# Loads of 48 and 40 partition rows are issued as loads of 32 and 8 rows in a gated linear recurrence kernel

## The chip, the core and the metric

The kernel runs on one core of a Trainium2 chip. A core has a matrix engine (PE, with its weight loads shown as PEld), a vector engine (DVE), a scalar engine (ACT), a general engine (POOL) and a queue engine (SP) that here does nothing but issue DMAs. The 16 DMA engines of the core carry all transfers between the chip's main memory and the on-chip memory of 128 partitions. The metric is the device time of one execution in microseconds (us).

## What is computed

The reference takes `r, k, v, w, a, b` of shape (4 batches, 8 heads, 768 steps, 40) and runs a recurrence over the steps, per batch and head, on a 40 x 40 state. The result goes through a small gated network.

```
for t in range(S):
    y[:, :, t] = einsum('bhd,bhde->bhe', rt, state)
    Sa = einsum('bhde,bhe->bhd', state, at)
    state = state * wt[:, :, None, :] - einsum('bhd,bhe->bhde', Sa, bt) \
            + einsum('bhd,bhe->bhde', vt, kt)
...
h = maximum(x @ w_in, 0);  u, v = halves of h
v_n = (v - mean) / sqrt(var + 1e-6)
out = (u * (w_spatial @ v_n + b_spatial)) @ w_out
```

## The kernel before

The 768 steps are cut into chunks of 64, and the four batches into two pairs, so that 24 chunks (numbered s or q, 0 to 23) run one after the other. A chunk holds 16 (batch, head) pairs. Eight of them lie on partitions 0 to 39 and eight on partitions 64 to 103, one partition for each of the 40 features; the code calls these two sets the halves, `par` 0 and 1.

For every chunk four inputs are loaded, all of them issued by SP:

- `ein` (line 556, `prep_load`): w, a, b and k of the chunk, 2064 numbers (8256 bytes) for each partition. There are two such tiles, used by turns. The host array has 64 rows for each half. Rows 40 to 63 hold constants (w is 1, the rest 0), and the vector engine's scans run over all 128 partitions. The loads of chunks 4 to 23 take 48 rows of each half. Those of chunks 0 to 3 are made another way at the start, and also fill the rows above 40 (or a memset does).
- `lin` (line 760, `lin_load`): v and r of the chunk, 40 rows for each half, 8 pieces of 512 bytes each.
- `lisw` (line 764): a part of r again, with the halves exchanged, 40 rows.
- `Rt` (line 768): v again in another layout, 64 rows.

The vector engine starts a chunk with `scan1` (line 569), a running product over w, which reads `ein`; `scan2` (578), `at` (596) and `sl` (602) read it too, after which the next load but one may overwrite the tile. PE first reads `lin` in `b_h` (line 816).

SP also issues the stores and reloads that carry results along: `scr` and `scn` (lines 590 and 923, decay factors between chunks), `xs` (1057, the recurrence's output), and, from about 270 us on, the transfers of the gated network, which runs interleaved with the later chunks: `xt` (1076 and 1080), `uts` (1160) and `vns` (1143).

The order of the instructions on every engine, SP included, is written out beforehand: a table of times sorts the steps, and each engine runs its list in that order. What stands behind a waiting instruction waits too. Each DMA adds to one of eight semaphores, DMAHW0 to DMAHW7, taken in rotation, and the program makes a DMA wait until the one issued eight places earlier has landed. So SP has at most eight transfers on their way.

Of the kernel before, what the change touches and what calls it, by code (L numbers as in the profile page):

```python
# [22 lines left out]
E = 40  # L23
# [8 lines left out]
LATE = 2 * C  # L32
# [465 lines left out]
def phase1(ctx, tc, early, late, vtok, win, xs, vns, uts, dscr):  # L498
    nc = tc.nc
# [4 lines left out]
    PR = (LO, HI)  # L504
    RR = (slice(0, E), slice(64, 64 + E))
    LV = slice(0, 64 + E)

    def pool(name, bufs=1, **kw):
        return ctx.enter_context(tc.tile_pool(name=name, bufs=bufs, **kw))
# [34 lines left out]
    lin = [linp.tile([P, NU, LATE + E], F32, name=f"lin{i}") for i in range(2)]  # L544
# [7 lines left out]
    def prep_load(s, rows, cols=slice(0, EW), i=None, queues=(nc.sync, nc.sync)):  # L552
        t = ein[s % 2 if i is None else i]
        for par in range(2):
            o = par * 64
            queues[par].dma_start(out=t[o:o + rows, cols], in_=early[par, s, 0:rows, cols])

    def scan1(s, i=None):
        t = ein[s % 2 if i is None else i]
        Et = etp.tile([P, WF], F32, name="Et")  # L560
        at = fifo[s % 8].tile([P, NU, C], F32, name="at")
        sl = fifo[s % 8].tile([P, NU, 2, C], F32, name="sl")
        wseg = t[:, 0:WF]
        oth = t[:, WF:].rearrange("p (q n c) -> p n q c", q=3, c=C)
        sx = pin.tile([P, WF], F32, name="S", bufs=2)
        sv = sx.rearrange("p (n c) -> p n c", c=WSEG)
        st["pre", s] = (Et, at, sl)
        st["raw", s] = (wseg, oth, sv)
        nc.vector.tensor_tensor_scan(  # L569
            out=sx[:, ::-1], data0=wseg[:, ::-1], data1=ends[:, ::-1],  # L570
            initial=0.0, op0=ALU.mult, op1=ALU.add,
        )
        nc.vector.reciprocal(out=eseg[:, :, 0:1], in_=sv[:, :, 1:2])

    def scan2(s):
        Et, at, sl = st["pre", s]
        wseg, oth, sv = st["raw", s]
        nc.vector.tensor_tensor_scan(
            out=Et, data0=wseg, data1=ends, initial=0.0, op0=ALU.mult, op1=ALU.add,
        )  # L580
# [11 lines left out]
    def at_mul(s, eng, ns=slice(0, NU)):  # L592
        Et, at, sl = st["pre", s]
        oth = st["raw", s][1]
        Ev = Et.rearrange("p (n c) -> p n c", c=WSEG)
        eng.tensor_tensor(out=at[:, ns], in0=oth[:, ns, 0], in1=Ev[:, ns, 0:C], op=ALU.mult)

    def sl_mul(s, eng, ns=slice(0, NU)):
        Et, at, sl = st["pre", s]
        wseg, oth, sv = st["raw", s]  # L600
        k = ns.stop - ns.start
        eng.tensor_tensor(  # L602
            out=sl[:, ns], in0=oth[:, ns, 1:],
            in1=sv[:, ns, 2:C + 2].unsqueeze(2).broadcast_to([P, k, 2, C]), op=ALU.mult,
        )
# [151 lines left out]

    def lin_load(s):
        for par in range(2):
            nc.sync.dma_start(out=lin[s % 2][RR[par], :, 0:LATE], in_=late[par, s])  # L760

    def lin_load_swapped(s):
        for par in range(2):
            nc.sync.dma_start(out=lisw[s % 2][RR[1 - par], :, 0:C], in_=late[par, s, :, NP:NU, C:2 * C])

    def vtok_load(s):
        for par in range(2):
            nc.sync.dma_start(out=Rts[s % 2][par][PR[1 - par], :, C:], in_=vtok[s, par])
# [243 lines left out]
    def c_mp_out(s, g):  # L1012
# [5 lines left out]
        mp = st["xx", g][:, :, C:]  # L1018
        sc = st["scn"][LV, g].rearrange("p e n -> p n e")
        if s in ADD_PE:  # L1020
            nc.vector.tensor_tensor(out=Mc[LV, gp, 0:E], in0=mp[LV], in1=sc, op=ALU.mult)
            return
        mn = Mc[:, gp, 0:E]
        nc.vector.tensor_tensor(out=mn[LV], in0=mp[LV], in1=Mc[LV, gp, 0:E], op=ALU.add)
        nc.vector.tensor_tensor(out=Mc[LV, gp, 0:E], in0=mn[LV], in1=sc, op=ALU.mult)

# [11 lines left out]
    def c_y_out(s, g):  # L1038
# [3 lines left out]
        if c % 2 == 0:  # L1042
# [3 lines left out]
        nc.vector.tensor_tensor(  # L1046
            out=y[LV, :, ys], in0=st["bp", g][LV, :, 0:C], in1=Ev[LV, gp, 0:C], op=ALU.mult,
        )
# [118 lines left out]
    def at(fn, *args, name=None):  # L1167
        plan.append((next(left[name or fn.__name__]) / 1e4, len(plan), fn, args))
# [46 lines left out]
    for q in range(GS, NS):  # L1215
        for fn in (scan1, scan2, scr_store, lprime, lblock):
            at(fn, q)
        at(at_mul, q, AT_ENG)
        at(sl_mul, q, SL_ENG)
        if q + 2 < NS:  # L1220
            at(prep_load, q + 2, 48)
    for g in range(1, NS // GS):
        gen = invert16(g) if g < N16 else invert(g)
        for k in range(INV_N[g]):
# [28 lines left out]
    def pads(eng, t):  # L1253
        w = t[:, 0:WF].rearrange("p (n c) -> p n c", c=WSEG)
        eng.memset(w[:, :, 1:C + 1], 1.0)
        eng.memset(w[:, :, 0:C + 2:C + 1], 0.0)
        eng.memset(t[:, WF:], 0.0)

    with tc.manual_schedule():
        W, O = slice(0, WF), slice(WF, EW)  # L1260
        qs = (nc.sync, nc.scalar)
        nc.vector.memset(eseg[:, :, 0:C + 1], 0.0)
        nc.vector.memset(eseg[:, :, C + 1:], 1.0)
        pads(v, ein[1])
        p.memset(maskl, -1.0)
        for q in range(P // HB):
            rows = slice(q * HB, (q + 1) * HB)
            p.affine_select(
                out=maskl[rows], in_=maskl[rows], pattern=[[1, HB]], base=0,
                channel_multiplier=-1, compare_op=ALU.is_gt, fill=0.0,  # L1270
            )
        pads(p, ein[2])
        pads(p, ein[3])
        for q in range(GS):
            for cols in (W, O):
                prep_load(q, 48 if q else 64, cols, q, qs)
        lin_load(0)
        lin_load_swapped(0)
        vtok_load(0)
        make_identity(nc, ident)  # L1280
        for t in (Mc, *xfs):
            p.memset(t, 0.0)
        for q in range(2):
            for rows in RR:
                diag = ident[rows, rows.start:rows.start + E]
                nc.scalar.activation(
                    lin[q][rows, :, LATE:], diag.unsqueeze(1).broadcast_to([E, NU, E]), AF.Copy
                )
                nc.scalar.activation(
                    lisw[q][rows, :, C:], diag.unsqueeze(1).broadcast_to([E, NP, E]), AF.Copy  # L1290
                )
        for q in range(GS):
            scan1(q, q)
            scan2(q)
            at_mul(q, v)
            sl_mul(q, v)
            scr_store(q)
            lprime(q)
            if q:
                lblock(q - 1)  # L1300
            if q == 0:
                b_copy(0, 0)
                b_copy(0, 1)
            if q == 1:
                b_lka(0)
                b_tok(0, 0)
                b_tok_out(0, 0)
            if q == 2:
                b_lka_out(0, 0)
                b_lka_out(0, 1)  # L1310
                b_tok(0, 1)
                b_tok_out(0, 1)
                b_l21(0)
                b_l21_out(0)
        lblock(GS - 1)
        lin_load(1)
        lin_load_swapped(1)
        vtok_load(1)
        prep_load(4, 48)
        prep_load(5, 48)  # L1320
        b_h(0)
        for _ in (invert16 if N16 else invert)(0):
            pass
        b_h_out(0, 0)
        b_h_out(0, 1)
        p.memset(lowrow, 1.0)
        p.memset(half, 0.0)
        for q in range(P // HB):
            rows = slice(q * HB, (q + 1) * HB)
            p.affine_select(  # L1330
                out=lowrow[rows], in_=lowrow[rows], pattern=[[0, 1]], base=-QB,
                channel_multiplier=1, compare_op=ALU.is_ge, fill=0.0,
            )
            for blk in range(2):
                cols = slice(blk * QB, (blk + 1) * QB)
                nc.scalar.activation(
                    half[rows, blk, cols], ident[rows, q * HB + blk * QB:q * HB + (blk + 1) * QB], AF.Copy,
                )
        open_fifo()
        st["dec"] = late_bufs.enter_context(tc.tile_pool(name="dec", bufs=1))  # L1340
        at(b_zt, 0)
        at(b_zt_out, 0)
        prep(0)
        at(b_x21, 0)
        at(b_x21_out, 0)
        plan.sort()
        anchors = {}
        n = 0
        while plan[n][0] < NS:
            t, _, fn, args = plan[n]  # L1350
            for a, _ in W_PLAN:
                if t >= a and a not in anchors:
                    anchors[a] = mark(nc)
            fn(*args)
            n += 1
# [59 lines left out]
```

## Time and profile before

| | |
|---|---|
| median of 3 runs | 685.62 us (680.43 to 688.12) |
| the profiled execution's own time | 683.68 us |
| its span, first to last instruction | 681.9 us |
| PE busy | 87% of the span |
| DVE busy | 77% |
| ACT, POOL busy | 62%, 32% |
| moved by DMA | 83.42 MB, mean 122 GB/s |
| mean granted PE clock | 0.885 of full speed |

The profile has several views. The page gives busy times, and the chain of work that ended last: from the last instruction it is followed back, at each step to what released it. The list of waits says which instruction waited for which. The view of a tile or line lists its instructions with their durations. The timeline gives instructions in order of time, with the idle time before them and its releaser in brackets. The view of stretches gives busy time, granted clock, DMA share and rate of a stretch. Times are us from the span's start; in the view of a tile, durations are in nanoseconds. SPq is SP's queue.

### The profile page before, as it was taken

What the parts mean: (1) busy time and instruction counts of PE and PEld (TensorE: products, weight loads), DVE (VectorE), ACT (ScalarE), POOL (GpSimd) and SP (SyncE); (2) the same over time, 40 slices, a digit from 0 to 9 for tenths busy, and PEclk for the clock granted to TensorE, in tenths of its full rate; (3) what the DMA queues carried; (4) which work ended last, traced back from release to release, by engine and by line L of the source; (5) the groups of instructions that cost most, each with busy time, mean ns of one, the idle gap of its engine ahead of it and who ended that gap; (6) DMA issues with size and microseconds to landing.
All of it is one profiled execution on the core that took longest, in us unless ns stands there. A gap on an engine that the chain in (4) does not pass through costs nothing.

```text
span 681.9 us, 27083 instructions
## 1 busy us (share of the span) xinstructions
PE 590.1 (87%) x11504; PEld 519.8 (76%) x11504; DVE 524.9 (77%) x1111; ACT 419.8 (62%) x934; POOL 215.1 (32%) x286
## 2 busy tenths in 40 slices
PE   1657888686889788889999989898998999999997
PEld 1546777575677677778788778687887999999997
DVE  7875148886897979889899878986849878777752
ACT  3334446473755877877787869786975644543422
POOL 3201112122345556543343224152413300512221
PEclk9975568787857899889899979997998999999999
DMA  9395424346554748265763464245445765435111
GB/s 184 62 159 93 115 54 78 89 104 131 88 144 93 136 99 164 46 145 124 175 157 99 109 192 124 90 120 153 123 127 169 219 205 160 124 115 159 47 59 58
DMA packets 115496, 83.42 MB, mean 122 GB/s; under 512 B 44656, under 2 KB 107376, under 8 KB 113456
## 3 DMA queue, kind: packets, MB, share of 16 engines
q1 hardware_dynamic: 114832, 79.98, 47.7%
q10 hardware_dynamic: 544, 1.72, 1.2%
q8 instruction: 90, 1.47, 1.0%
q14 instruction: 30, 0.25, 0.2%
HBM read 61.16 MB, written 20.50 MB: 120 GB/s over the span
## 4 chain that ended last, share of the span: by engine, by line
PE 50%; DVE 19%; DMA 12%; ACT 7%; issue 6%; SPq 4%; POOL 1%; DVEq 0%; ACTq 0%; POOLq 0%
PE pg L423 9%; PE po L478 6%; DMA ein<-in_early 4%; PE ch L956 4%; PE pv L1153 4%; PE pv L1107 3%; PE bp L939 3%; DMA vns<-vr 3%; PE ch L977 2%; PE bk L816 2%; PE bk L838 2%; PE bk L786 2%; PE bp L1033 2%; PE bk L875 2%; PE ch L1007 2%
## 5 line engine op out<-in xcount | busy, mean ns | idle before, releaser
L793 POOL TENSOR_SCALAR_AFFINE_SELECT Rt<-Rt 64x256 f32<-64x256 f32 (+1 forms) x144 | 89.0, 618 | 184.1 <-ACT Rt L988 96.7
L793 POOL TENSOR_SCALAR_AFFINE_SELECT At<-At 64x512 f32<-64x512 f32 x48 | 40.7, 849 | 117.6 <-ACT At L803 116.3
L216 POOL TENSOR_TENSOR gl<-g,gh 128x384 fp32r<-128x384 f32 x32 | 34.3, 1077 | 106.8 <-ACT gh L212 106.8
L948 ACT ACTIVATE Rt<-bp 64x416 f32<-64x416 f32 x96 | 49.0, 511 | 18.1 <-PE bp L939 16.3
L650 DVE TENSOR_TENSOR itmp<-A 128x84 f32<-128x84 f32 (+12 forms) x130 | 55.9, 430 | 3.3
L956 PE MATMUL ch<-Rt,At 128*64 128x104 f32 x768 | 55.9, 295 | 2.7 <-issue 2.3
L988 ACT ACTIVATE Rt<-ch 64x416 f32<-64x416 f32 x96 | 49.0, 511 | 13.5 <-PE ch L977 11.6
L956 PEld LDWEIGHTS ch<-Rt,At 128*64 128x64 f32 x768 | 45.7, 163 | 10.4 <-issue 6.0
L654 DVE TENSOR_TENSOR A<-A,itmp 128x84 f32<-128x84 f32 (+12 forms) x130 | 45.0, 346 | 4.5
L838 PE MATMUL bk<-ident,sl 128*128 128x128 f32 x192 | 35.2, 313 | 9.1 <-DVE Lc L626 7.0
L569 DVE TENSOR_TENSOR_SCAN S<-ein,ends 128x528 f32<-128x528 f32 x24 | 31.3, 1304 | 11.5 <-DMA ein<-in_early 7.7
L615 PE MATMUL bk<-at,sl 64*32 64x32 f32 x1536 | 22.5, 217 | 19.1 <-DVE sl L602 15.6
L786 PE MATMUL bk<-at,sl 64*64 64x64 f32 x768 | 35.8, 258 | 1.4 <-issue 0.8
L615 PEld LDWEIGHTS bk<-at,sl 64*32 64x32 f32 x1536 | 19.7, 128 | 22.2 <-DVE sl L602 14.2
L826 ACT ACTIVATE Rt<-bk 64x512 f32<-64x512 f32 x48 | 28.2, 588 | 12.2 <-PE bk L816 11.1
L786 PEld LDWEIGHTS bk<-at,sl 64*64 64x64 f32 x768 | 32.6, 170 | 4.1 <-issue 2.3
L816 PE MATMUL bk<-lin 40*64 40x64 f32 x768 | 31.2, 236 | 4.5 <-issue 4.5
L1033 PE MATMUL bp<-Rt,tk 128*40 128x64 f32 x768 | 34.0, 239 | 0.7 <-issue 0.3
L803 ACT ACTIVATE At<-bk 64x512 f32<-64x512 f32 x48 | 28.2, 589 | 10.2 <-PE bk L786 9.4
L1033 PEld LDWEIGHTS bp<-Rt,tk 128*40 128x40 f32 x768 | 27.4, 130 | 8.5 <-issue 6.1
L838 PEld LDWEIGHTS bk<-ident,sl 128*128 128x128 f32 x192 | 23.1, 154 | 13.7 <-issue 7.2
L212 ACT ACTIVATE gh<-g 128x384 fp32r<-128x384 f32 x32 | 16.2, 519 | 27.3 <-DVE g L429 27.2
(183 smaller groups left out, 1765.1 us busy)
## 6 DMA issues: line engine op xcount, KB each, us to landing
ein<-in_early SPq DMA_DIRECT2D x40, 387.0 KB
lin<-in_late SPq DMA_DIRECT2D x48, 160.0 KB
uts<-ur SPq DMA_DIRECT2D x48, 128.0 KB
vns<-vr SPq DMA_DIRECT2D x24, 256.0 KB
raw<-vns SPq DMA_DIRECT2D x48, 128.0 KB
ut<-uts SPq DMA_DIRECT2D x48, 128.0 KB
Rt<-in_vtok SPq DMA_DIRECT2D x48, 80.0 KB
xs<-y SPq DMA_DIRECT2D x48, 80.0 KB
```

What stands on the lines that cost most here:

```text
L423: nc.tensor.matmul(pg, lhsT=x[:, i], rhs=y[i][:, w], start=first and i == 0 and n == 0, stop=i == KT - 1 and n == 2, skip_group_check=True,)
L615: nc.tensor.matmul(pl[o:o + HB, n, :], lhsT=sl[PR[par], n, par, cs], rhs=at[PR[par], n, cs], start=True, stop=True,)
L650: nc.vector.tensor_tensor(out=tp, in0=A[:, k + 1:, k:k + 1].broadcast_to([P, m, k]), in1=A[:, k:k + 1, 0:k].broadcast_to([P, m, k]), op=AL ...
L654: nc.vector.tensor_tensor(out=A[:, k + 1:, 0:k], in0=A[:, k + 1:, 0:k], in1=tp, op=ALU.add)
L786: nc.tensor.matmul(pk[PR[1 - par], n, :], lhsT=sl[PR[par], n, 1 - par, :], rhs=at[PR[par], n, :], start=True, stop=True,)
L793: nc.gpsimd.affine_select(out=t, in_=t, pattern=[[0, k], [1, C]], base=0, channel_multiplier=-1, compare_op=ALU.is_gt, fill=0.0,)
L816: nc.tensor.matmul(ph[PR[1 - par], n, :], lhsT=li[RR[par], n, 0:C], rhs=li[RR[par], n, C:2 * C], start=True, stop=True,)
L838: nc.tensor.transpose(pt[:, n, :], sl[:, h * NP + n].rearrange("p q c -> p (q c)"), ident)
L948: nc.scalar.activation(Rt[par][PR[par], gp, :], st["bp", g][PR[par]], AF.Copy)
L956: nc.tensor.matmul(ff[PR[1 - par], q, :], lhsT=At[par][:, n, :], rhs=Rt[par][:, n, :], start=True, stop=True,)
L988: nc.scalar.activation(Rt[par][PR[par], gp], xx[PR[1 - par ^ flip(s, g)]], AF.Copy, scale=-1.0)
L1033: nc.tensor.matmul(bp[RR[par], q, 0:C], lhsT=tk[:, n, par, :], rhs=Rt[par][:, n, 0:C], start=False, stop=True, skip_group_check=True,)
```

## The change

For chunks 4 to 23, each half's 48-row load of `ein` becomes two: rows 0 to 31, and rows 32 to 39. Rows 40 to 47 are no longer loaded; they keep the constants that the start has put there. For all 24 chunks, each half's 40-row load of `lin` becomes two in the same way. So a chunk has four issues for `ein` where it had two, and four for `lin` where it had two. The loads of chunks 0 to 3 of `ein` stay as they are (the call only passes the rows as a slice).

```
+    ROWS = (slice(0, 32), slice(32, E))
...
         for par in range(2):
             o = par * 64
-            queues[par].dma_start(out=t[o:o + rows, cols], in_=early[par, s, 0:rows, cols])
+            for r in rows:
+                queues[par].dma_start(out=t[o + r.start:o + r.stop, cols], in_=early[par, s, r, cols])
...
     def lin_load(s):
         for par in range(2):
-            nc.sync.dma_start(out=lin[s % 2][RR[par], :, 0:LATE], in_=late[par, s])
+            for r in ROWS:
+                o = slice(par * 64 + r.start, par * 64 + r.stop)
+                nc.sync.dma_start(out=lin[s % 2][o, :, 0:LATE], in_=late[par, s, r])
...
-            at(prep_load, q + 2, 48)
+            at(prep_load, q + 2, ROWS)
...
-                prep_load(q, 48 if q else 64, cols, q, qs)
+                prep_load(q, (slice(0, 48 if q else 64),), cols, q, qs)
...
-        prep_load(4, 48)
-        prep_load(5, 48)
+        prep_load(4, ROWS)
+        prep_load(5, ROWS)
```

On PE, DVE, ACT and POOL the same instructions stand in the same order as before; only what they wait for differs. On SP the order is the same but for the added issues, 88 in all. The change's file is two lines longer at 556 (558 there) and four lines longer from 764 on.

The first place is SP's list where the loads of `lin` for chunk 1 and of `ein` for chunks 4 and 5 stand, at about 30 to 39 us. Before:

```order
14 L760 DMA lin_137<-in_late 40x8x128 x2
15 L764 DMA lisw_139<-in_late 40x4x64 x2
16 L768 DMA Rt_134<-in_vtok 64x8x40
17 L768 DMA Rt_135<-in_vtok 64x8x40
18 L556 DMA ein_120<-in_early 48x2064 x2
19 L556 DMA ein_121<-in_early 48x2064 x2
20 L764 DMA lisw_138<-in_late 40x4x64 x2
```

With the change:

```order
17 L764 DMA lin_137<-in_late 32x8x128
18 L764 DMA lin_137<-in_late 8x8x128
19 L764 DMA lin_137<-in_late 32x8x128
20 L764 DMA lin_137<-in_late 8x8x128
21 L768 DMA lisw_139<-in_late 40x4x64 x2
22 L772 DMA Rt_134<-in_vtok 64x8x40
23 L772 DMA Rt_135<-in_vtok 64x8x40
24 L558 DMA ein_120<-in_early 32x2064
25 L558 DMA ein_120<-in_early 8x2064
26 L558 DMA ein_120<-in_early 32x2064
27 L558 DMA ein_120<-in_early 8x2064
28 L558 DMA ein_121<-in_early 32x2064
```

Two issues of `lin` have come in ahead of the first load of chunk 4, and between the two halves of each chunk of `ein` there is one issue more.

The second place is SP's list from the load of `ein` for chunk 21, at about 303 to 311 us, with the semaphores that each issue waits for. Before:

```order
253 L556 DMA ein_121<-in_early 48x2064 [waits DMAHW4_49,DVE_49]
254 L556 DMA ein_121<-in_early 48x2064 [waits DMAHW5_49]
255 L1057 DMA xs<-y_4782 40x4x128 [waits DMAHW6_49,DVE_49]
256 L1057 DMA xs<-y_4782 40x4x128 [waits DMAHW7_49]
257 L1160 DMA uts<-ur 128x256 [waits DMAHW0_49,Activation_49]
258 L1057 DMA xs<-y_4784 40x4x128 [waits DMAHW1_49,DVE_49]
259 L1057 DMA xs<-y_4784 40x4x128 [waits DMAHW2_49]
260 L923 DMA scn<-scr 64x320 [waits DMAHW3_49]
261 L923 DMA scn<-scr 64x320 [waits DMAHW4_49]
262 L1160 DMA uts<-ur 128x256 [waits DMAHW5_49,Activation_49]
263 L760 DMA lin_136<-in_late 40x8x128 [waits DMAHW6_49,PE_49]
```

With the change:

```order
315 L558 DMA ein_121<-in_early 32x2064 [waits DMAHW2_49,DVE_49]
316 L558 DMA ein_121<-in_early 8x2064 [waits DMAHW3_49]
317 L558 DMA ein_121<-in_early 32x2064 [waits DMAHW4_49]
318 L558 DMA ein_121<-in_early 8x2064 [waits DMAHW5_49]
319 L1061 DMA xs<-y_4840 40x4x128 [waits DMAHW6_49,DVE_49]
320 L1061 DMA xs<-y_4840 40x4x128 [waits DMAHW7_49]
321 L1164 DMA uts<-ur 128x256 [waits DMAHW0_49,Activation_49]
322 L1061 DMA xs<-y_4842 40x4x128 [waits DMAHW1_49,DVE_49]
323 L1061 DMA xs<-y_4842 40x4x128 [waits DMAHW2_49]
324 L927 DMA scn<-scr 64x320 [waits DMAHW3_49]
325 L927 DMA scn<-scr 64x320 [waits DMAHW4_49]
326 L1164 DMA uts<-ur 128x256 [waits DMAHW5_49,Activation_49]
```

Before, the second `scn` and the second `uts` wait for the two loads of `ein` to land. Now the four issues from the last `xs` to the second `uts` wait for its four loads; the `uts` still waits for the last of them.

The third place is PE's list where `b_h` of chunk 2 reads `lin`. Before:

```order
168 L1007 MATMUL ch<-tk,Rt_135 40x40
169 L816 MATMUL bk<-lin_136 64x64 [waits DMAHW7_49,PE_49,Activation_49]
170 L816 MATMUL bk<-lin_136 64x64 [waits DMAHW0_49]
171 L816 MATMUL bk<-lin_136 64x64 x14
172 L1001 MATMUL ch<-Mc,ident 40x4x40 [waits Activation_49]
```

With the change:

```order
168 L1011 MATMUL ch<-tk,Rt_135 40x40
169 L820 MATMUL bk<-lin_136 64x64 [waits DMAHW0_49,DMAHW7_49,PE_49,Activation_49]
170 L820 MATMUL bk<-lin_136 64x64 [waits DMAHW2_49,DMAHW1_49]
171 L820 MATMUL bk<-lin_136 64x64 x14
172 L1005 MATMUL ch<-Mc,ident 40x4x40 [waits Activation_49]
```

Each half of `lin` is now waited for on two semaphores where it was one.

## Rows read from the trace of the kernel before

**Rows 1.** The page: span, busy times, chain by engine

```profile
span 681.9 us, 27083 instructions
...
PE 590.1 (87%) x11504; PEld 519.8 (76%) x11504; DVE 524.9 (77%) x1111; ACT 419.8 (62%) x934; POOL 215.1 (32%) x286
...
PE 50%; DVE 19%; DMA 12%; ACT 7%; issue 6%; SPq 4%; POOL 1%; DVEq 0%; ACTq 0%; POOLq 0%
```

**Rows 2.** The chain that ended last: start, us, what

```profile
36.35 7.07 DMA ein<-in_early
...
144.68 6.63 DMA ein<-in_early
```

**Rows 3.** The list of waits: us in total, times, longest us

```profile
ACT vr L1113 <- DMA vns<-vr: 13.8, 8, 3.4
...
DVE S L569 <- DMA ein<-in_early: 7.7, 4, 2.7
```

**Rows 4.** Timeline of DVE, first scans of chunks 4 and 5: start, us

```profile
43.54 1.26 DVE L569 TENSOR_TENSOR_SCAN S<-ein,ends 128x528 f32<-128x528 f32 x1 [2.71 <-DMA ein<-in_early]
...
48.47 1.26 DVE L569 TENSOR_TENSOR_SCAN S<-ein,ends 128x528 f32<-128x528 f32 x1
```

**Rows 5.** Two stretches; the last three columns are PEclk, DMA share, GB/s

```profile
36.70:48.40 11.70, 6.65 (x193) 5.66 (x190) 8.58 (x15) 2.97 (x8) 1.38 (x2) 0.80 1.02 160
390.30:395.00 4.70, 4.67 (x136) 3.85 (x134) 2.43 (x9) 2.35 (x6) 2.21 (x5) 1.00 0.82 230
```

**Rows 6.** Tiles ein, lin, scr, lisw: SP's issues, min/median/max in ns

```profile
L556 SPq DMA_DIRECT2D ein<-in_early x48: 310/413/1500, 0.8 to 350.3; - x48
...
L760 SPq DMA_DIRECT2D lin<-in_late x48: 763/814/2022, 13.5 to 477.5; - x48
...
L590 SPq DMA_DIRECT2D scr<-sc x88: 272/331/1668, 20.6 to 388.7; - x88
...
L764 SPq DMA_DIRECT2D lisw<-in_late x48: 288/342/1630, 15.3 to 476.2; - x48
```

**Rows 7.** Timeline of SP, 30 to 38 us

```profile
30.67 1.64 SPq L760 DMA_DIRECT2D lin<-in_late  x2
...
35.75 1.94 SPq L556 DMA_DIRECT2D ein<-in_early  x4
```

**Rows 8.** Timeline of SP, 303 to 326 us

```profile
303.09 1.65 SPq L556 DMA_DIRECT2D ein<-in_early  x2
...
307.71 1.17 SPq L923 DMA_DIRECT2D scn<-scr  x2
310.05 0.40 SPq L1160 DMA_DIRECT2D uts<-ur  x1
310.54 1.76 SPq L760 DMA_DIRECT2D lin<-in_late  x2
...
325.19 0.57 SPq L1143 DMA_DIRECT2D vns<-vr  x1
```

**Rows 9.** Timeline of ACT, two evictions of the gated network

```profile
329.66 0.60 ACT L1113 ACTIVATE vr<-pv 128x512 f32<-128x512 f32 x1 [2.35 <-DMA vns<-vr]
...
396.09 0.60 ACT L1113 ACTIVATE vr<-pv 128x512 f32<-128x512 f32 x1 [3.38 <-DMA vns<-vr]
```

**Rows 10.** Timeline of SP, 348 to 390 us

```profile
348.04 1.70 SPq L760 DMA_DIRECT2D lin<-in_late  x2
349.78 2.04 SPq L556 DMA_DIRECT2D ein<-in_early  x2
...
354.71 1.72 SPq L1080 DMA_DIRECT2D xt<-xs  x2
357.95 1.24 SPq L768 DMA_DIRECT2D Rt<-in_vtok  x2
...
389.74 2.57 SPq L1143 DMA_DIRECT2D vns<-vr  x1
```

**Rows 11.** Line 816: the wait instructions of PE's queue, min/median/max in ns

```profile
L816 PEldq EVENT_SEMAPHORE  x22: 51/51/107, 27.6 to 486.5; - x22
```

**Rows 12.** Timeline of PE: a pause that nothing in the profile explains

```profile
51.39 0.21 PE L728 MATMUL bk<-XT 32*16 32x16 f32 x2 [4.39 <-issue]
```

## Prediction

> **What bounds the kernel now.** I read the page first: PE is busy for 87% of a span of 681.9 us, and of the chain that ended last half is PE, 12% DMA, 6% "issue" (time in which an engine waits for nothing that the profile shows) and 4% SP's queue [rows 1]. The change touches nothing that PE, DVE, ACT or POOL compute, so it can act only through those last three shares. The chain says where DMA counts: two loads of `ein` stand in it after the start, of 7.07 and 6.63 us [rows 2]. The list of waits sizes it from the other end: DVE's first scan waits for `ein` for 7.7 us in all, four times [rows 3], the longest at chunk 4 (2.71 us) [rows 4]. No compute engine waits in that list for a landing of `lin`. A second wait hangs on SP indirectly: ACT waits 13.8 us, eight times, until a store of `vns` has landed and its tile is free again [rows 3], and those stores are issued by SP behind everything else in its list. So there are two questions: does a chunk of `ein` land sooner, and does SP come later to what others wait for?
>
> **The transfers of `ein`.** A chunk moves 2 x 40 rows instead of 2 x 48, so five sixths of the bytes. The lower bound of the time is that it scales with them. The best place to see what limits it is the stretch in which the four loads of chunks 4 and 5 drain: 11.7 us, DMA engines busy throughout (share 1.02), 160 GB/s. In the stretch in which a 768 KB load over all 128 partitions (a part of `w_spatial`) and a few stores run, a share of 0.82 moves 230 GB/s [rows 5]. Busy time for each byte is (1.02/160) / (0.82/230) = 1.8 times as high for `ein`. So these loads are slow neither for the number of bytes nor because engines stand idle, but for where they write, and partitions 0 to 39 are written with the change exactly as before. I take no gain; the bound on the good side is a sixth of the burst, 11.7 / 6 = 1.95 us at chunks 4 and 5, and a sixth of 6.63, 1.1 us, at chunk 12. At two places where SP waits for `ein` to land (310.05 and 357.95, below) and at chunk 6 it would be some 0.5 us each. Together -4.6 us. On the bad side I allow +0.5 us, since the last of four loads is issued later than the last of two.
>
> [...]
>
> **SP's issues.** An issue that is added costs SP its own duration. The nearest rows are the stores of 40 rows of 16 bytes (median 331 ns, minimum 272) and `lisw` (342 ns); the 48-row load of `ein` takes 413 ns [rows 6]. Four issues of `ein` in a row take 1.94 us, which is 0.1 us a gap above 4 x 0.413 [rows 7]. So 0.33 + 0.07 = 0.4 us for an 8-row issue (0.3 to 0.5), 0.8 us a chunk for `ein`; I leave the 32-row part at the 48-row price. For `lin` a half costs 0.814 us. The 32-row part lies between `lisw` (342 ns, the same 40 rows with a quarter of the bytes) and this; by rows it is 0.65, so a half goes from 0.81 to 0.65 + 0.05 + 0.33 = 1.03 us, and a chunk gains 0.4 us (-0.2 to +0.9). Over 20 and 24 chunks SP has 26 us more to do. Most of that falls where SP waits for a compute engine anyway. It counts where SP runs without a pause towards something that is waited for; I find three such places.
>
> *Chunks 4 and 5.* SP runs from the load of `lin` at 30.67 straight into the four loads at 35.75 [rows 7]; the added issues of `lin` put them 0.4 us later, and chunk 4's scan, which waits 2.71 us for them, too [rows 4]. The loads' own added issues hide under 11.7 us of transfer. PE's pause of 4.39 us [rows 12] ends after the same burst and moves with it, not on top. **+0.4 us** (-1.6 to +1.4).
>
> *303 to 330 us.* From 303.09 SP is busy up to the store of `vns` at 325.19, but for 310.05 - (307.71 + 1.17) = 1.17 us in which it waits, eight places behind chunk 21's load, for that load to land [rows 8]. The wait takes up `ein`'s 0.8 us; `lin` at 310.54 adds 0.4. ACT then waits 2.35 us for that store [rows 9], so all of the delay is seen. Between 0.4 and 1.2: **+0.6 us**.
>
> *348 to 396 us.* Here the issues of `lin` at 348.04 and `ein` at 349.78 come first; before 357.95 SP waits 1.52 us for chunk 23's load to land [rows 10], which again takes up `ein`'s 0.8. From there to the store of `vns` at 389.74 it never pauses, and two more loads of `lin` stand between. ACT waits 3.38 us for the store [rows 9]. Three times 0.4: **+1.2 us** (0 to 2.7).
>
> Elsewhere I cost the issues at nothing, because SP stands waiting behind them: its list has long waits for ACT, DVE and PE. Where that cover is gone a chunk costs 0.8 or 0.4 us.
>
> **Waits of PE and DVE.** `b_h` waits on two more semaphores a chunk, 48 in all. A wait instruction ahead of it takes 51 ns of PE's queue [rows 11], so at most 2.4 us, and nothing where the queue runs ahead. I take **+0.5 us**. DVE's added waits stand behind a running instruction and cost nothing.
>
> **The sum** is 0.4 + 0.6 + 1.2 + 0.5 = +2.7 us on the profiled execution's 683.7 us, so 686.4. That execution is 1.9 us below the median of 685.6; on the median it is 688.3, and I predict 688.
>
> **The rivals.** *The transfers scale with bytes.* For it: the DMA engines are saturated in the burst. Against it: the factor of 1.8 [rows 5]. Time: 685.6 + 2.7 - 4.6 = 683.7.
>
> *SP's queue counts in full.* From 258 us on SP is nearly always busy, and the eight places hold it back more when a chunk's loads take eight of them (four and four) instead of four. Six loads of `ein` and eight of `lin` are issued between 258 and 410 us: 6 x 0.8 + 8 x 0.4 = 8.0 us, or 12.0 at the upper price of `lin`. Against it: the waits of 1.17 and 1.52 us. With the other places' 0.9 that gives 694.5 to 698.5.
>
> *PE's pauses shrink: the other side.* The chain has 6% of "issue", 41 us [rows 1], and the longest pause seen, 4.39 us, ends 3 us after the burst of four loads has drained [rows 12, 5]. If what PE waits for there comes through the same DMA engines, it comes sooner when fewer rows are queued ahead. A sixth of 41 us is 6.8, which with the costs gives 685.6 + 2.7 - 6.8 = 681.5. It decides for "faster" from a quarter on: 10.2 us, 678.1. [...]
>
> **How the numbers follow.** No measurable change around +2.7 us: 0.55. Bytes: 0.15. SP in full: 0.18. PE's pauses: 0.12. About 1% (6.9 us) is what a measurement of this kernel can tell from no change; its three runs span 7.7 us. Slower by more than 1% is the SP rival and the edge of the first case: 0.23. Faster is a part of the last rival and of the bytes: 0.12. The rest, 0.65, lies within 1%. The range goes from 680, below both favourable cases' times, to 697, inside the SP rival.
>
> **What would show it.** Chunk 4's scan still about 5 us ahead of chunk 5's, as now (43.54 and 48.47 [rows 4]); a share near 1 but about 135 GB/s in that burst (5/6 of the bytes in the same time): no gain from bytes. An issue of 8 rows at 0.3 to 0.4 us, and of 32 rows of `lin` clearly below 0.8. ACT's waits for `vns` longer by 0.5 to 1.2 us. I would be wrong if chunk 5's scan came 1.5 us closer, if SP's pauses between 300 and 400 us vanished, or if the pauses of PE changed by more than 5 us in all.

## The result, and the profile after

| | before | after |
|---|---|---|
| median of 20 runs each | 679.99 us | 677.86 us |
| ratio after / before, 95% interval | | 0.990 (0.9852 to 0.9947) |
| span of the profiled execution | 681.9 us | 677.0 us |
| PE busy | 590.1 us | 579.1 us |

The changed kernel is faster, by 1.0% (6.8 us) by the ratio, where I had forecast no change that can be measured, with a tendency to slower. The ratio compares the undisturbed executions alone, and only 7 of the 20 after count as such; over all 20 and 20 the medians are 2.1 us and the means 2.8 us apart, so the size of the gain is open between some 2 and 7 us. The median of before is 5.6 us lower over 20 runs than over the three that I started from; of the 10 us between forecast and result that is the larger half. The rest, 4.5 us, is my reasoning.

The page after: the span, the busy times, the chain of work that ended last by engine.

```profile
span 677.0 us, 27217 instructions
...
PE 579.1 (86%) x11504; PEld 510.2 (75%) x11504; DVE 528.4 (78%) x1111; ACT 419.9 (62%) x934; POOL 215.2 (32%) x286
...
PE 55%; DVE 22%; DMA 8%; issue 6%; ACT 5%; SPq 3%; ACTq 0%; DVEq 0%
```

Against [rows 1], DMA has gone from 12% to 8% of the chain, "issue" has stayed at 6%, and PE is busy 11 us less for the same 11504 matmuls. That difference alone shows little: in the kernels below that gain nothing, PE is busy for 571.5 to 586.8 us. The list of waits after (us in total, times, longest us) answers [rows 3]:

```profile
ACT vr L1117 <- DMA vns<-vr: 13.4, 7, 4.1
...
DVE d_t L226 <- DMA raw<-in_wout: 7.7, 3, 4.8
...
DVE S L571 <- DMA ein<-in_early: 7.0, 4, 2.0
...
PE bk L820 <- DMA lin<-in_late: 1.6, 2, 1.1
```

The first scans still wait 7.0 us for `ein` where they waited 7.7 us. This wait, the only one of a compute engine by which I valued the transfers, has hardly changed. The first scans of chunks 4 to 7 on DVE (start us, us), to set beside [rows 4]:

```profile
42.66 1.26 DVE L571 TENSOR_TENSOR_SCAN S<-ein,ends 128x528 f32<-128x528 f32 x1 [1.99 <-DMA ein<-in_early]
...
47.50 1.25 DVE L571 TENSOR_TENSOR_SCAN S<-ein,ends 128x528 f32<-128x528 f32 x1
...
54.02 1.26 DVE L571 TENSOR_TENSOR_SCAN S<-ein,ends 128x528 f32<-128x528 f32 x1 [2.04 <-DMA ein<-in_early]
...
59.31 1.26 DVE L571 TENSOR_TENSOR_SCAN S<-ein,ends 128x528 f32<-128x528 f32 x1 [1.78 <-DMA ein<-in_early]
```

The scans of chunks 6 and 7 before:

```profile
55.16 1.26 DVE L569 TENSOR_TENSOR_SCAN S<-ein,ends 128x528 f32<-128x528 f32 x1 [2.21 <-DMA ein<-in_early]
61.61 1.26 DVE L569 TENSOR_TENSOR_SCAN S<-ein,ends 128x528 f32<-128x528 f32 x1 [2.93 <-ACT sc L587]
```

Chunk 4's scan comes 0.9 us earlier than before, and that of chunk 7 2.3 us earlier. SP's timeline around them answers [rows 7]:

```profile
30.30 3.49 SPq L764 DMA_DIRECT2D lin<-in_late  x4
...
36.10 3.11 SPq L558 DMA_DIRECT2D ein<-in_early  x8
...
47.60 1.40 SPq L558 DMA_DIRECT2D ein<-in_early  x4
```

Four issues of `lin` take 3.49 us where two took 1.64, over four times the 0.4 us that I had added; yet the first load of `ein` comes only 0.35 us later, because `lin` starts 0.37 us earlier and the two issues of `lisw` in between take 0.87 us where they took 1.98. The eight issues of `ein` take 0.39 us each. The stretches from 37.05 to 46.95 us, in which these loads drain, and from 40 to 100 us (the last three columns are PEclk, DMA share, GB/s):

```profile
37.05:46.95 9.90, 5.61 (x189) 4.82 (x185) 7.57 (x14) 2.49 (x7) 1.39 (x2) 0.67 0.87 163
...
40.00:100.00 60.00, 43.04 (x1421) 36.61 (x1422) 31.49 (x44) 27.72 (x66) 10.64 (x16) 0.63 0.50 91
```

The burst runs at 163 GB/s where it ran at 160 [rows 5], so it is 1.8 us shorter: 9.9 us for 11.7. I had expected the old length at 135 GB/s. The second row is the more important one. Before, the same stretch read:

```profile
40.00:100.00 60.00, 42.72 (x1294) 36.38 (x1292) 27.95 (x37) 24.97 (x61) 8.63 (x14) 0.56 0.54 100
```

In these 60 us PE gets through 1421 matmuls instead of 1294, in about the same busy time: 30.3 ns each instead of 33.0, at a granted clock of 0.63 instead of 0.56. These are two executions; what the other kernels' traces show in the same stretch stands with f1 below.

### The profile page after: what moved, and what is told of

It is laid out like the page before. It is cut to its first block, busy times and chain, and to the rows that moved or that the text cites. A ratio compares the mean times of both kernels' runs of the same rounds, so it can differ in the third digit from the quotient of the medians.

```text
span 677.0 us, 27217 instructions
## 1 busy us (share of the span) xinstructions
PE 579.1 (86%) x11504; PEld 510.2 (75%) x11504; DVE 528.4 (78%) x1111; ACT 419.9 (62%) x934; POOL 215.2 (32%) x286
## 4 chain that ended last, share of the span: by engine, by line
PE 55%; DVE 22%; DMA 8%; issue 6%; ACT 5%; SPq 3%; ACTq 0%; DVEq 0%
PE pg L423 12%; PE po L478 6%; PE pv L1111 4%; PE ch L960 4%; PE pv L1157 4%; DVE itmp L652 3%; PE bp L943 3%; DMA ein<-in_early 3%; DVE A L656 3%; PE bp L1037 2%; PE bk L842 2%; PE ch L981 2%; PE bk L820 2%; PE bk L790 2%; DMA vns<-vr 2%
## 5 line engine op out<-in xcount | busy, mean ns | idle before, releaser
L960 PE MATMUL ch<-Rt,At 128*64 128x104 f32 x768 | 54.2, 291 | 2.4 <-issue 2.1
L992 ACT ACTIVATE Rt<-ch 64x416 f32<-64x416 f32 x96 | 49.0, 510 | 11.1 <-PE ch L981 9.2
L943 PE MATMUL bp<-lin,Mc 40*64 40x104 f32 x384 | 28.5, 293 | 9.8 <-DVE y L1050 8.7
L820 PEld LDWEIGHTS bk<-lin 40*64 40x64 f32 x768 | 27.5, 146 | 10.3 <-issue 6.6
L1157 PE MATMUL pv<-xh,wh 128*128 128x256 f32 x123 | 26.1, 319 | 10.4 <-ACT vr L1117 6.5
L617 PEld LDWEIGHTS bk<-at,sl 64*32 64x32 f32 x1536 | 18.3, 120 | 21.7 <-DVE sl L604 14.1
L212 ACT ACTIVATE gh<-g 128x384 fp32r<-128x384 f32 x32 | 16.2, 518 | 27.0 <-DVE g L429 27.0
L423 PE MATMUL pg<-wsh,ls 128*128 128x384 f32 x96 | 32.4, 337 | 0.6 <-DVE ls L216 0.6
```

The source lines that it names most:

```text
L423: nc.tensor.matmul(pg, lhsT=x[:, i], rhs=y[i][:, w], start=first and i == 0 and n == 0, stop=i == KT - 1 and n == 2, skip_group_check=True,)
L820: nc.tensor.matmul(ph[PR[1 - par], n, :], lhsT=li[RR[par], n, 0:C], rhs=li[RR[par], n, C:2 * C], start=True, stop=True,)
L943: nc.tensor.matmul(st["bp", g][PR[par], q, :], lhsT=Mc[rows, n, :], rhs=rhs, start=(q == 0), stop=False, skip_group_check=True,)
L960: nc.tensor.matmul(ff[PR[1 - par], q, :], lhsT=At[par][:, n, :], rhs=Rt[par][:, n, :], start=True, stop=True,)
L992: nc.scalar.activation(Rt[par][PR[par], gp], xx[PR[1 - par ^ flip(s, g)]], AF.Copy, scale=-1.0)
L1157: nc.tensor.matmul(pu, lhsT=l, rhs=r, start=(j == 0), stop=(j == len(mm) - 1))
```

## The experiments

Every ratio is against runs of the kernel before on the same chip; the us are the ratio's distance from 1 times the median of before there (681 to 683 us). Differences named in the expectations are of means or medians over all executions and so differ: little in most, but 6.5 us for e2 and 13 us for g3. e7, f2, f3 and g3 leave inputs out and compute with constants in their place.

| run | kernel | ratio (95%) | us |
|---|---|---|---|
| e1 | ein 32 + 8, lin as before | 0.9869 (0.9806 to 0.9931) | -8.9 |
| e2 | lin 32 + 8, ein as before | 1.0042 (0.9986 to 1.0098) | +2.9 |
| e3 | ein 40 in one load | 0.9838 (0.9772 to 0.9903) | -11.1 |
| e4 | ein 32 + 16 (48 rows) | 1.0012 (0.9965 to 1.0059) | +0.8 |
| e5 | ein 40, chunks 4 to 7 only | 0.9920 (0.9881 to 0.9958) | -5.5 |
| e6 | ein 40, chunks 8 to 23 only | 0.9888 (0.9834 to 0.9942) | -7.6 |
| e7 | ein 8 | 0.9667 (0.9610 to 0.9723) | -22.7 |
| e8 | lin 32 + 8, chunk 1 only | 1.0034 (0.9988 to 1.0080) | +2.3 |
| f1 | w first, chunks 4 to 7, 48 rows | 1.0025 (0.9988 to 1.0062) | +1.7 |
| f2 | ein 8, chunks 4 to 7 only | 0.9883 (0.9829 to 0.9937) | -8.0 |
| f3 | ein 32 | 0.9722 (0.9668 to 0.9776) | -18.9 |
| f4 | ein 40, w first in chunks 4 to 7 | 0.9784 (0.9727 to 0.9841) | -14.7 |
| g1 | lin 32 + 8, chunks 16 to 23 only | 1.0047 (1.0006 to 1.0087) | +3.2 |
| g2 | lin 32 + 8, chunks 2 to 15 only | 0.9983 (0.9936 to 1.0029) | -1.2 |
| g3 | ein 8 in eleven chunks nobody waits for | 0.9863 (0.9818 to 0.9909) | -9.3 |
| g4 | four idle copies | 1.0033 (0.9986 to 1.0079) | +2.2 |
| h1 | 22 idle copies, 7.2 MB | 1.0054 (1.0015 to 1.0093) | +3.7 |
| h2 | ein 64 in the eleven chunks | 1.0068 (1.0036 to 1.0101) | +4.6 |

**The parts of the change.** e1 leaves `lin` alone, e2 `ein`.

```
 e1: prep_load(.., ROWS)          lin_load as before
 e2: prep_load(.., 48) as before  lin_load over ROWS
```

> Only the 48-row loads of ein become 32 + 8; lin stays as before. Theory 1 (the shorter transfers of ein are the gain, the issues of lin are a cost): as fast as the whole change or a little faster, 3 to 6 us below before; chunk 4's first scan starts 6.6 us after the first issue of its ein, as in the whole change (36.10 to 42.66), and not 7.8 us as before (35.75 to 43.54). Rival (lin's smaller pieces are the gain): no difference to before. Rival (nothing has changed but the order of PE's pauses): 0, within 2 us.

> Only the 40-row loads of lin become 32 + 8; ein keeps its 48 rows in one load. Theory 1: 0 to 2 us slower than before, since SP gets 48 issues more and nothing that is waited for lands sooner; chunk 4's first scan 7.8 us after the first issue of ein. Rival (lin's smaller pieces are the gain): 3 us faster.

Theory 1 holds: the whole gain is `ein`'s, and `lin`'s split costs, if anything. -8.9 and +2.9 add up to -6.0, near the whole change's -6.8. (The profiled execution of e1 took 773.4 us at a mean granted clock of 0.651, and is not read here.)

**Fewer rows or another cut.**

```
 e3: ROWS = (slice(0, E),)
 e4: ROWS = (slice(0, 32), slice(32, 48))
```

> The loads of ein have 40 rows in one issue instead of 48, with no split; lin stays as before. Theory 1a (the dropped rows are what makes the transfer shorter): chunk 4's first scan 6.6 us after the first issue, the time as in the run that splits ein alone, 3 to 6 us below before. [...]

> The loads of ein keep all their 48 rows, but in two issues of 32 and 16 rows; lin stays as before. Theory 1a (the dropped rows): chunk 4's first scan 7.8 to 8.2 us after the first issue, the time that of before or up to 2 us above it (40 issues more on SP). Theory 1b (the split): 6.6 us, and 3 us faster.

It is the dropped rows. With 48 rows in two pieces nothing is gained, and 40 more issues of SP cost at most 4 us; with 40 rows in one piece the gain is at least that of the change. In size theory 1 was far off: 11 us, not 3 to 6. From the first issue of chunk 4's `ein` to its scan it is 7.8 us before, 7.4 in e2, 7.6 in e4, 7.0 in e3 and 6.6 after, in the sense of theory 1a; but it is a weak sign, since other kernels with 48 rows there lie between 7.1 (h2) and 10.2 us (e6). In the drain of chunks 4 and 5 in e3 the engines are, on average, not busy throughout:

```profile
36.65:46.80 10.15, 6.11 (x193) 5.15 (x190) 7.81 (x15) 2.93 (x8) 1.39 (x2) 0.67 0.68 162
```

The rate is 162 GB/s, as before, at a DMA share of 0.68 instead of 1.02. So the mean share does not tell what limits the rate.

**Where the gain arises.**

```
 e5: prep_load(s, 40 if s < 8 else 48)
 e6: prep_load(s, 48 if s < 8 else 40)
 e7: prep_load(s, 8)
```

> 40 rows in one load for chunks 4 to 7 alone, where the first scans wait for ein; chunks 8 to 23 keep 48 rows, lin stays as before. Theory 1 (the gain is the scans' wait for ein, so it arises up to 66 us): about 1 us at chunk 7's scan, and less than 3 us in all, of the 12 us that 40 rows in all chunks gave. Theory 2 (what is earlier there grows later: PE's clock and the transfers behind it): 6 us or more from these four chunks alone.

> 40 rows in one load for chunks 8 to 23 alone; chunks 4 to 7 keep 48 rows. Theory 3 (the bytes that are no longer moved clear the way for the other transfers, at many places): 8 us or more of the 12 us. Theory 1 (the scans' wait for ein, which stands at chunk 12 alone after 66 us): 1 to 2 us.

> Each load of ein for chunks 4 to 23 takes 8 rows instead of 48 (rows 8 to 39 keep the constants, so w, a, b and k of chunks 4 to 23 are left out but for 8 features), lin stays as before. A bound on what ein's transfers cost: no issue is added, 5/6 of their bytes are gone. Theory 1: the waits of the first scans are gone (7.7 us in the trace) and some 8 to 12 us of the time. Theory 3 (cost in proportion to the bytes): 12 us for 8 rows of 48, so 40 us or more.

Four chunks of twenty give 5.5 us (theory 2 rather than 1), the other sixteen 7.6 us, though behind 66 us the scan of one chunk alone waits. Theory 3 is right in that many places count, but not in proportion to the bytes: 8 rows less give 11.1 us, and 32 rows less again only 11.6 us more.

**Is it the scans' wait?** f1 takes that wait away and moves all the bytes.

```
+    def prep_cols(s, rows):
+        for cols in (slice(0, WF), slice(WF, EW)):
+            prep_load(s, rows, cols)
```

> All 48 rows and all bytes of ein as before, but for chunks 4 to 7 each half's load is cut by columns: first the 2112 bytes of w for both halves, then the 6144 bytes of a, b and k. The first scan reads w alone, so DVE's wait for ein at chunks 4 and 6 gets shorter, while the DMA engines have as much to move as before. Theory 1 (the gain of 40 rows in chunks 4 to 7, 5.9 us, is the scans' shorter wait): 3 to 6 us faster. Theory 4 (it is PE's pauses, of which those from 40 to 100 us add up to 10.8 us in the trace of before and 8.8 us with 40 rows in chunks 4 to 7: what PE waits for queues behind ein's rows): 0, within 2 us, and pauses of 10 to 13 us.

Theory 1 falls here. The scans of chunks 4 and 6 do start without a wait, chunk 6's 4.4 us before the 55.16 us that it had:

```profile
41.44 1.21 DVE L573 TENSOR_TENSOR_SCAN S<-ein,ends 128x528 f32<-128x528 f32 x1
...
50.76 1.25 DVE L573 TENSOR_TENSOR_SCAN S<-ein,ends 128x528 f32<-128x528 f32 x1
...
57.73 1.26 DVE L573 TENSOR_TENSOR_SCAN S<-ein,ends 128x528 f32<-128x528 f32 x1 [3.46 <-ACT sc L591]
```

Chunk 7 waits for ACT, as it did before, and is still 3.9 us earlier (57.73 for 61.61 us); yet the time does not fall. In the stretch from 40 to 100 us of f1 PE has got hardly further than before:

```profile
40.00:100.00 60.00, 42.77 (x1328) 36.39 (x1324) 30.04 (x40) 25.14 (x61) 9.73 (x14) 0.60 0.55 101
```

The same stretch of e5 (40 rows in chunks 4 to 7) and of f3 (32 rows, below):

```profile
40.00:100.00 60.00, 45.02 (x1508) 38.59 (x1508) 32.25 (x44) 27.96 (x66) 9.74 (x16) 0.66 0.45 101
```

```profile
40.00:100.00 60.00, 47.75 (x1592) 40.92 (x1594) 37.55 (x53) 31.33 (x75) 12.21 (x18) 0.68 0.41 90
```

PE's count in this stretch goes with the rows. In the ten traces of kernels that load no fewer rows than before (before itself, e2, e4, e8, f1, g1, g2, g4, h1, h2) it is 1291 to 1402, in the nine that load fewer (after, e3, e5, e6, e7, f2, f3, f4, g3; e6 and g3 from chunk 8 on) it is 1421 to 1629. The count says how far PE has come, and not why. The mean time of a matmul overlaps: 29.7 to 33.0 ns in the ten, of which before is the highest, 28.7 to 30.9 in the nine; so does the clock, 0.56 to 0.67 and 0.63 to 0.72. So what after does faster than before in the same busy time can't be put down to the rows from these two traces. Over the whole span the nine have, on average, PE busy for 5.7 us less than the ten and not busy for 6.5 us less. The granted clock, as a mean over all executions, was 0.897 to 0.903 for the kernel before in the sessions of these runs; it was 0.914 to 0.920 in e3, e7, f3, f4 and g3, but 0.902 in e5 and 0.896 in f2, which gain 5.5 and 8.0 us without it.

Theory 4, that PE's pauses of kind "issue" shrink, is borne out in part only. The pauses of over 0.9 us between 40 and 100 us in the chain add up to 10.8 us before, 14.0 us in f1 and 9.7 us in g2, which load 48 rows; to 9.3 us after, 11.4 in e3, 8.8 in e5, 9.9 in f4; to 5.0 in f3 and 5.4 in e7. So they go with the rows, but from 48 to 40 rows by no more than they vary from one execution to the next: in the ten traces they add up to 9.5 to 15.5 us, in the nine to 3.3 to 11.4.

**How the time goes with the rows.**

```
 f2: prep_load(s, 8 if s < 8 else 48)
 f3: prep_load(s, 32)
```

> 8 rows of ein in chunks 4 to 7 (rows 8 to 39 keep the constants there, so most of w, a, b and k of these four chunks is left out), 48 rows in chunks 8 to 23. The bound on what these four chunks' transfers cost. Theories 1 and 4 alike: 10 to 15 us of the 23 us that 8 rows in all chunks gave, with pauses of PE from 40 to 100 us of some 5 to 6 us in all; proportion to the bytes (four chunks of twenty): 4 to 5 us.

> Each load of ein for chunks 4 to 23 takes rows 0 to 31 (rows 32 to 39 keep the constants, so a fifth of w, a, b and k is left out there). If the time of a transfer follows its bytes at the 160 GB/s seen in the burst of chunks 4 and 5, that burst ends 2.1 us earlier than with 40 rows, and the time lies between the 12 us that 40 rows gave and the 23 us of 8 rows: some 14 to 16 us below before. [...]

f2: chunks 4 to 7 hold some 8.0 us (4.3 to 11.6), less than the 10 to 15 of theories 1 and 4, and 40 rows already give 5.5 of it. f3: 8 rows less than e3 give another 7.8 us, so the step from 40 to 32 rows is large. The burst of chunks 4 and 5 shows it: in f3 it takes 6.6 us, where e3 took 10.15, at 207 GB/s for 162:

```profile
36.28:42.90 6.62, 4.85 (x136) 4.01 (x137) 6.24 (x14) 3.07 (x8) 0.65 (x1) 1.00 0.96 207
```

That is shorter than four fifths of e3's, 8.1 us, which is what bytes alone would give. A single transfer shows it at chunk 6, whose scan waits for it in the kernels compared here. Before, the scan starts at 55.16 us, 6.67 us after SP's issue:

```profile
48.49 1.62 SPq L556 DMA_DIRECT2D ein<-in_early  x2
```

In e3 and in f3:

```profile
47.66 0.68 SPq L558 DMA_DIRECT2D ein<-in_early  x2
```

```profile
54.49 1.26 DVE L571 TENSOR_TENSOR_SCAN S<-ein,ends 128x528 f32<-128x528 f32 x1 [2.46 <-DMA ein<-in_early]
```

```profile
45.57 0.80 SPq L556 DMA_DIRECT2D ein<-in_early  x2
```

```profile
50.12 1.26 DVE L569 TENSOR_TENSOR_SCAN S<-ein,ends 128x528 f32<-128x528 f32 x1 [0.18 <-DMA ein<-in_early]
```

48 rows take 6.67 us, 40 rows 6.83 us, 32 rows 4.55 us; 32 + 8 rows (after, 47.60 to 54.02) take 6.42 us. Between 48 and 40 rows no difference can be told: the other kernels with 48 rows there, where the scan waits, have 6.3 to 8.0 us. So for a chunk that drains by itself the prediction was right that 40 rows take as long as 48; with four loads in the queue the burst got shorter by the bytes (11.70 us before, 10.15 in e3, 9.90 after). Why 32 rows land sooner than either is not shown.

**A version that beats both.**

```
 f4: ein_40, and prep_cols for chunks 4 to 7
```

> 40 rows of ein in one load in chunks 8 to 23, and in chunks 4 to 7 40 rows cut by columns as in the run that loads w first; lin as before. A version meant to beat both kernels. Theory 1: 3 us or more below 40 rows alone, so 15 us below before. Theory 4: that of 40 rows alone, 12 us below before.

14.7 us below before, and below the changed kernel by the intervals (0.9727 to 0.9841 against 0.9852 to 0.9947). Against e3 the 3.6 us lie inside both intervals.

**Where `lin`'s split costs.**

```
 e8: for r in (ROWS if s == 1 else (slice(0, E),))
 g1: ... if s >= 16
 g2: ... if 2 <= s < 16
```

> lin's load becomes 32 + 8 for chunk 1 alone, right ahead of the loads of ein for chunks 4 and 5; everything else as before. Theory A (the cost of lin's split, 6.5 us when all 24 chunks have it, arises at this place, which chunk 4's scan waits behind): 1.3 us later at chunk 4's scan, and 3 us or more in all. Theory B (it arises from SP's queue at the later chunks): 0 to 1.5 us.

> lin's load becomes 32 + 8 for chunks 16 to 23 alone (issued from about 200 us on, beside the gated network's transfers); everything else as before. Theory B (the 6.5 us that lin's split costs in all chunks arise where SP's queue has no pause): 4 to 7 us slower. If they arise earlier: 0 to 2 us.

> lin's load becomes 32 + 8 for chunks 2 to 15 alone. Theory B: 0 to 2 us slower, since SP stands waiting behind these issues. If the cost arises here: 4 us or more.

Only the late chunks cost by more than the interval, +3.2 us (0.4 to 5.9), a little below what theory B gave; for the middle ones no cost is seen (-4.4 to 2.0). Chunk 1 alone (+2.3, -0.8 to 5.5) stays undecided, but theory A's sign is missing: chunk 4's scan starts at 43.20 us in e8, no later than before. One place in the late chunks can be seen: after, SP's queue ahead of a load of `w_out`, and DVE, which waits for it:

```profile
451.46 3.65 SPq L764 DMA_DIRECT2D lin<-in_late  x4
455.22 1.14 SPq L927 DMA_DIRECT2D scn<-scr  x2
456.41 0.92 SPq L1061 DMA_DIRECT2D xs<-y  x2
457.37 1.36 SPq L221 DMA_DIRECT2D raw<-in_wout  x1
```

```profile
461.33 0.33 DVE L226 TENSOR_SCALAR d_t<-raw 128x320 int32<-128x320 int32 x1 [4.76 <-DMA raw<-in_wout]
```

Before, the two issues of `lin` there took 1.70 us, and the same instruction on DVE waited 1.97 us:

```profile
464.71 0.33 DVE L226 TENSOR_SCALAR d_t<-raw 128x320 int32<-128x320 int32 x1 [1.97 <-DMA raw<-in_wout]
```

In e2 and g1, which have the split there, the wait is 4.86 and 4.22 us; in e3, e8 and g2, which do not, 2.24 to 2.38 us. So up to 2 to 2.8 us of the cost may stand here, if DVE's wait counts in full, which no run shows by itself.

**Transfers that nobody waits for.** FREE is 8, 9, 13 to 15, 17 to 19, 21 to 23.

```
 g3: prep_load(s, 8 if s in FREE else 48)
 g4: + nc.sync.dma_start(out=dump[s], in_=early[0, s, 0:48])         # s in 7..10
 h1: + nc.sync.dma_start(out=dump[s][par], in_=early[par, s, 0:E, 0:2048])  # s in FREE
 h2: prep_load(s, 64 if s in FREE else 48)
```

> 8 rows of ein instead of 48 in the eleven chunks whose first scan came 7 us or more after the landing in the trace of before (8, 9, 13 to 15, 17 to 19, 21 to 23), 48 rows in the others; the left-out rows keep the constants, so those chunks' w, a, b and k are left out but for 8 features. No scan waits for these transfers. Theory 5 (a transfer costs time beyond the wait for it: what is queued behind its rows, PE's pauses among it, comes later): 6 to 12 us faster. Rival (only waits for ein count): 0, within 2 us.

> Everything as before, and behind the loads of ein for chunks 7, 8, 9 and 10 one copy more of 396 KB within main memory that nothing reads; the next load of ein is 4 us or more behind each but for chunk 7's. Theory 5: 2 to 6 us slower, and PE's pauses from 40 to 100 us above the 10.8 us of before. Rival (only waits for ein count): 0 to 1 us, the price of four issues.

> Everything as before, and behind the loads of ein in the eleven chunks where no scan waits for them (8, 9, 13 to 15, 17 to 19, 21 to 23) two copies more of 40 rows of 8192 bytes within main memory, which nothing reads: 7.2 MB in all, as much as the run with 8 rows in these chunks left out (7.3 MB). Theory 5a (the DMA engines' time counts: whatever is queued behind rows comes later): 10 us slower or more, as that run was 13 us faster. Theory 5b (it is the writing into the partitions of ein that counts, not the engines' time): 0 to 3 us.

> 64 rows of ein instead of 48 in those eleven chunks (rows 48 to 63 bring the constants that stand there already), 2.9 MB more in all, no issue added. In proportion to the 40 rows less that gave 13 us, 16 rows more cost 5 us. [...]

g3 is the plainest: 9.3 us (6.2 to 12.4) from transfers for which no scan waits. In its list of waits the scans wait even longer for `ein` than the 7.7 us of [rows 3]:

```profile
DVE S L569 <- DMA ein<-in_early: 9.6, 5, 3.6
```

Theory 5 holds, its rival falls. One more wait could be meant, that of SP for landings of `ein`, eight places back. Added up from the list of SP's waits it is 14.7 us before and 10.9 in g3, so it gives 3.8 of the 9.3 us at most; in e3 it is 16.2 us, so it gives nothing of the 11.1. What it is that these rows hold up is less clear. Copies within main memory cost too: 3.7 us (1.0 to 6.3) for 7.2 MB in h1, less than half of what 7.3 MB of `ein` gave in g3. A part of that may be the price of its 22 issues, since 40 more in e4 cost 4 us at most. For the four of g4 (+2.2, -1.0 to 5.4) a cost can't be told, though PE's pauses there, 15.5 us, are the most of all the traces. 2.9 MB more into the partitions in h2 cost 4.6 us (2.5 to 6.9), more than those 7.2 MB. So neither theory holds alone: by the middle values what is written into the partitions of `ein` counts two to three times as much for each byte as a copy (1.6 us per MB in h2 and 1.3 in g3, 0.5 in h1), though the intervals just touch. Which transfer or fetch is held up, I have not shown; nor have I tested whether the constants that take the place of inputs in g3, f3, f2 and e7 matter. e3, f4 and h2 compute with all inputs and go the same way.

## Why the prediction was wrong, step by step

**"It can act only through those last three shares"** of the chain, and the transfers of `ein` are worth the waits for them. This is the step that failed, and the term "I take no gain". The waits for `ein` barely moved (7.7 to 7.0 us), as I said; but starting the scans earlier gained nothing (f1), and transfers for which no scan waits are worth 9.3 us (g3). The term that I put at nothing measured 8.9 us in e1 and 11.1 in e3. My bound for it, -4.6 us, was built from waits too, and so it didn't hold them. PE was counted as a share that the change can't touch; in every trace with fewer rows it gets more done between 40 and 100 us (1421 to 1629 matmuls against 1291 to 1402). By which way the rows reach it is open: shorter pauses, the clock and waits of other engines may each be a part. The chain also has a third load behind the start, which I had passed over when I wrote of two [rows 2]:

```profile
108.16 6.46 DMA ein<-in_early
```

It goes on from there through ACT's line 587 and SP's stores, and not through a scan.

**Partitions 0 to 39 are written as before, so the transfer takes as long.** Nearly right for one chunk (6.67, 6.83 and 6.42 us at chunk 6), wrong for the burst of four loads, which ran at 163 GB/s as before (160) and so ended with its bytes. That these loads are slow for where they write was my inference from the factor of 1.8 [rows 5]; the runs show that loads of 32 rows land sooner than the bytes would give (4.55 us at chunk 6 for 6.83 with 40 rows; 207 GB/s in the burst for 162), and not by what. The sign that I named for it was badly chosen: chunk 5's scan follows chunk 4's by 4.84 us after as by 4.93 before, but that is DVE's own work on chunk 4, and tells nothing of the landing.

**SP's issues.** For `ein` right: 8 + 32 rows cost 0.7 us at chunk 6 (1.40 for 0.68 in e3), and e4 puts all 40 at 0.8 us (-2.4 to 4.0). For `lin` mis-sized: I took the 8-row part at the price of other small stores. Four issues take 3.49 and 3.65 us where two took 1.64 and 1.70. The tile `lin` after, SP's issues:

```profile
L764 SPq DMA_DIRECT2D lin<-in_late x96: 567/701/1842, 12.9 to 475.0; - x96
```

96 at a median of 701 ns are 67 us; 48 at 814 ns were 39 [rows 6]. That is 1.2 us a chunk, not 0.4.

**The three places of SP.** At chunks 4 and 5 the issue came 0.35 us later, near the 0.4 that I had summed; that is luck, since the issues of `lin` took 1.85 us more and other waits gave it back, and chunk 4's scan came earlier all the same. ACT's two waits for the store of `vns` [rows 9] after:

```profile
322.04 0.60 ACT L1117 ACTIVATE vr<-pv 128x512 f32<-128x512 f32 x1 [3.90 <-DMA vns<-vr]
...
388.66 0.60 ACT L1117 ACTIVATE vr<-pv 128x512 f32<-128x512 f32 x1 [4.10 <-DMA vns<-vr]
```

They are 1.55 and 0.7 us longer; I had 0.6 and 1.2. All of ACT's waits for these stores together did not grow (13.8 us before, 13.4 after). A fourth place, the load of `w_out` at 457 us, I had not looked for, since it lies behind the last load of `ein`; its wait has grown by 2.8 us, more than the other two together. SP's waits for a landing of `ein` I took at two places, 2.7 us; the list has 14.7 us at 13 places. As a whole, `lin`'s +2.9 us is near the +2.2 us of the three places, by an interval (-1.0 to 6.7) too wide to say more.

**PE's added waits.** The wait instructions at line 820 are 55 of 51 ns where there were 22 [rows 11], 1.7 us of PE's queue in all; no run here tells what of it counts. DVE's at its first scan, which I took at nothing, are 38 with a median of 50 ns (longest 1.17 us) where there were 24 with one of 21 ns; DVE's queue is 0% of the chain before and after.

**The rivals.** "SP's queue counts in full" gave 8 us and more; it doesn't. "The transfers scale with bytes" had the rate right in the burst and its price from the waits wrong. "PE's pauses shrink" came nearest, with a chance of 0.12: it named PE's side, and its 681.5 and 678.1 us are near the 677.9 measured; but the pauses can explain a part at most, and nearly half of what the nine traces gain over the ten is in PE's busy time, which it had left out. None of my three signs of being wrong could have told: chunk 5's scan kept its distance, SP still pauses between 300 and 400 us, and "issue" in the whole chain fell by 3 us only (6.4% to 6.0% of the span).

**Open:** what PE waits for in the pauses that the profile calls "issue", how much of the gain is the clock, and whether it follows PE's work or leads it, and what else is held up in the later chunks.

## What to carry to other kernels

A transfer's price need not be the wait for it (g3: 9.3 us from loads that no scan waits for): before costing a load at nothing because nobody waits, look at what else runs in its stretch, above all at how far the busiest engine gets there over several traces, and try it by leaving out rows of loads that have slack. Row counts need not count by the bytes: here 32 rows of a half took 4.55 us at chunk 6, from SP's issue to the scan, where 40 took 6.83 and 48 took 6.67, and 40 in one issue was at least as good as 32 + 8 (-11.1 us in e3, -8.9 in e1). Splitting `lin`, a load of many short pieces, doubled its issues without halving their price (two took 1.64 us, four 3.49); in the late chunks, where SP's queue has few pauses (before, one of 1.17 us between 303.09 and 325.19 us [rows 8]), a part of that was paid (g1: some 9.4 us more of issues, 3.2 us of time).

## What the runs showed of the hardware

- A stretch with 40-row loads moved 162 GB/s at a DMA share of 0.68 (e3), one with 48-row loads 160 GB/s at 1.02, one with 32-row loads 207 GB/s at 0.96 (f3): here the share says little of what limits the rate.
- Load of one chunk of 8256-byte rows at chunk 6: 6.67 us with 48 rows a half, 6.83 with 40, 4.55 with 32.
- PE's granted clock is 0.50 in some stretches (75 to 80 us before) and 1.00 in others (390.30 to 395.00 us before [rows 5], 90 to 95 us after), and it changes at different times in different executions: in the five microseconds from 75 us, before and after,

```profile
75.00:80.00 5.00, 5.00 (x93) 3.83 (x89) 1.21 (x3) 2.45 (x5) 1.31 (x2) 0.50 0.01 3
```

```profile
75.00:80.00 5.00, 3.64 (x187) 3.26 (x184) 0.05 (x1) 2.27 (x5) 0.05 (x1) 0.84 0.65 145
```

  after, it is 0.84 on average, and PE does twice the matmuls in less busy time (187 in 3.64 us for 93 in 5.00); but from 80 to 85 us both are at 0.50 again, and the matmuls are not the same ones. That fewer rows bring the higher clock about is not shown.
